# Expert inputs of a routed MoE: turned by VectorE after a round trip through HBM instead of by TensorE

## The chip, the cores and the metric

One NeuronCore of a Trainium2 chip runs the whole program. The metric is device time in microseconds (us). The kernel before took a median of 859.29 us over three runs (854.42 to 859.76).

The engines are named as the profile names them: PE is TensorE (matrix products; PEld its weight loads), DVE is VectorE, ACT is ScalarE, POOL is GpSimd, SP is SyncE. SP only issues DMAs here. A name with a q (SPq) is the instruction queue of that engine. Every engine works through its own instructions in the order in which the program wrote them; an instruction that waits holds up all that stand behind it on that engine.

## The reference

First an attention with a sigmoid in place of a softmax, then a mixture of eight experts to which the tokens are dealt out by a global sort.

```python
scores = scale * np.matmul(q, k.transpose(0, 1, 3, 2)) - np.log(S)     # batch 8, heads 12, S 448, head_dim 64
attn = 1.0 / (1.0 + np.exp(-scores)); x = attn @ v                      # as rows: 3584 tokens x 768
order = np.argsort(-(x @ w_gate).flatten())                             # E = 8 experts, cap = 3584 // 8 = 448
for idx in order:                                                       # best pair of token and expert first
    tok, e = idx // E, idx % E
    if assigned[tok] >= 0 or counts[e] >= cap: continue
    assigned[tok] = e; counts[e] += 1
for e in range(E):
    mask = assigned == e
    out[mask] = np.maximum(x[mask] @ w1[e], 0.0) @ w2[e]                # w1 768x1024, w2 1024x768
```

Each expert therefore gets exactly 448 tokens.

## The kernel before

**Stages.** The attention runs first and writes its result, one row of 768 numbers per token, to an HBM tensor `xs`. Within a row the columns stand in a permuted order (a, r, j): 4 quarters a, 6 blocks r, 32 columns j. Then come the eight experts in the order in which they fill up. "Expert k" below is the k-th of that order, counted from 0.

**An expert** (`moe`, from L833) is 288 products on PE, and a few more for experts 0 and 7. All numbers are split into a high and a low part in fp32r, so that each product of a pair takes three matmuls: high by high, low by high, high by low. The first half (products 0 to 143, L853 to L857) has the x of the expert as the moving operand, `xh` and `xl`, 448 tokens wide, with the features on the partitions. The second half (products 144 to 287, L890 to L894) has the hidden layer as the moving operand. The very first product of an expert reads all 448 columns of `xh`, the second all of `xl`.

**The weights** come in units, 8 in the first half and 6 in the second. SP loads a unit three units ahead (`load_w`), ACT rounds it to its high part (L709), POOL subtracts to get the low part (L711; VectorE does every second one from unit 84 on, which is in expert 6). POOL also makes the low part of the hidden layer (L865).

**x of the next expert.** Once the list of its 448 tokens is known, `prepare` puts these steps on the list of chores: four gathers of up to 128 rows of `xs` on POOL (`gather`, L731); a copy on ACT that puts a row's columns in order (`order`, L740); and eight `xturn`s. Each `xturn` is three 128x128 transposes on PE into PSUM (L757), a rounding copy to `xh` on ACT (L760), and a subtraction on VectorE to `xl` (L761). The fourth block of tokens has 64 rows.

**y of an expert** leaves PSUM by a VectorE transpose (`turn_y`, L787), is stored to an HBM tensor by SP (L793), read back in rows by SP (L797) and scattered to the output by POOL (`scatter`, L809), all in the course of the next expert.

**The router** finds the next expert and its tokens while an expert runs. `phase` is a generator: keys, a transpose on PE (`ends`, L178), nine steps of a search on VectorE (`grid_search`: each counts the keys over three thresholds, L185 to L240), then `prove` (PE transposes and counts, L289 and L290; VectorE reads a value into its sequencer and branches on it, L302, to an exact search of 16 passes if the count isn't 448), `choose`, `place` (L333 to L344) and `lists` (L356 to L374, with 32 small matmuls at L365). For expert 0 the search has four steps with a matmul in each (L230), and nothing else runs beside it.

**The order of the work** is written out by the program itself. A clock counts 189 ns for each product that is issued (L764). Each `yield` of the router names the time after which its next part is issued; SLACK, 150 ns, is added. Each chore has a due time; one chore is issued at a time, at least 1000 ns apart, the first of the list that is due. A due time of t is therefore a place in the stream of products: product t/189 of the expert. When an instruction really runs is decided by its engine's queue and by what it waits for.

The buffers that matter: `xr` has 12 (rows gathered and rows of y in turn), `xq` 2, `xh` and `xl` 2 each, the raw and split weights 4 each, the product's PSUM tile 2.

Of the kernel before, what the change touches and what calls it, by code (L numbers as in the profile page):

```python
# [7 lines left out]
F32 = mybir.dt.float32  # L8
# [23 lines left out]
T_GRID, T_PROVE, T_FOUND = (0, 2290, 3600, 3600, 3600, 3600, 3600), 3000, 9000  # L32
# [6 lines left out]
Y_WAIT, Y_LATE = 5000, 26000  # L39
N_FIRST, N_FAST = 4, 9  # L40
PAD = 176
NONE = 1.0e30
FOUND = 0x43E00000
ORDER = 2500

# [83 lines left out]
class Router:  # L129
# [217 lines left out]
    def lists(self):  # L347
# [13 lines left out]
        yield T_OH  # L361
# [38 lines left out]
    def phase(self, k):  # L400
        if k:
            self.remove()
        if k < 7:
            self.keys()
            yield T_KEYS
            self.ends()
            yield from self.grid_search(k)
            yield T_PROVE
            self.prove(k)
            yield T_FOUND  # L410
        else:
            self.left()
            yield T_PICK
        yield from self.place()
        yield from self.lists()


def moe_attention(tc, q, k, v, w_gate, w1, w2, out):
# [7 lines left out]
    with contextlib.ExitStack() as ctx:  # L426
# [14 lines left out]
        ys = [dr.tile([S, DM], F32, name=f"ys{i}") for i in range(2)]  # L441
        K = Consts()
# [118 lines left out]
        def scale():  # L561

            a = rw.tile([128, CP], F32, name="s_a", bufs=1)
            nc.vector.tensor_scalar(a.bitcast(I32), LE[:, 0].bitcast(I32), 0x7FFFFFFF, None, OP.bitwise_and)
            m = rw.tile([128, 2], F32, name="s_m", bufs=1)
            nc.vector.tensor_reduce(m[:, :1], a, AX.X, OP.max)
            p = ps_t.tile([128, 512], F32, name="tp")
# [9 lines left out]
            nc.vector.tensor_scalar(K.T0, K.kw[:, 0], K.base0, None, OP.add)  # L577

# [30 lines left out]
        for i in range(NPR + 1):  # L609
# [26 lines left out]
            if old and old[1] == NP - 1:  # L636
# [3 lines left out]
                if b == 3:  # L640
                    bg.append(scale)
# [81 lines left out]
        xg, xq, XH = {}, {}, {}  # L723
# [9 lines left out]

        def order(kx, j, n):

            xq[kx, j] = xp.tile([128, DM], F32, name="xq", bufs=2)
            to = xq[kx, j][:n].rearrange("p (r a j) -> p r a j", r=ND, j=32)
            of = xg[kx, j][:n].rearrange("p (a r j) -> p r a j", r=ND, j=32)
            if kx:
# [42 lines left out]
        def turn_y(kx, i, py, yr):  # L782
# [17 lines left out]
            if i == (2 if kx < E - 1 else 1):  # L800
                for j, n in blocks():
                    chores.append((clock[0] + 2 * wait, kx + 2, lambda j=j, n=n: rows_back(j, n)))
                for j, n in blocks() if kx < E - 1 else ():
                    chores.append((clock[0] + (Y_LATE if kx < E - 2 else 4 * wait) + 2000 * j, kx + 2,
# [133 lines left out]
        t_route, t_chore = FIRST, 1500.0  # L938
        for kx in range(E):
# [3 lines left out]
            def prepare():  # L943
                t0 = clock[0]
                lag = max(ORDER + 5000, min(14000, start + 40000 - t0))
                for j, n in blocks():
                    if kx:
                        chores.append((t0 + 1500 * j, kx + 1, lambda j=j, n=n: gather(kx + 1, j, n)))
                    else:
                        gather(1, j, n)  # L950
                bl = list(blocks())
                chores.append((t0 + lag - ORDER, kx + 1, lambda: order(kx + 1, *bl[0])))
                for i, (j, n) in enumerate(bl):
                    def first(i=i, j=j, n=n):
                        xturn(kx + 1, j, n, 0, False)
# [3 lines left out]
                    chores.append((t0 + lag + 1500 * j, kx + 1, lambda j=j, n=n: xturn(kx + 1, j, n, 1, False)))  # L959
# [6 lines left out]
            for step, cost in enumerate(moe(kx)):  # L966
# [4 lines left out]
                if t >= t_route:  # L971
# [43 lines left out]
```

## Time and profile before

| | |
|---|---|
| median of 3 runs | 859.29 us |
| the profiled execution: its time | 858.42 us |
| its span, first to last instruction | 856.6 us |
| mean granted TensorE clock | 0.978 of full speed |
| PE busy | 93% of the span |
| VectorE busy | 59% |
| POOL busy | 54% |
| ACT busy | 48% |

The profile is of one execution. "Busy" leaves out register, branch, semaphore and DMA-issuing instructions. Matmuls overlap: a product of 448 columns is shown with about 0.36 us, while the next one starts 0.20 us after it. So the distance from start to start is what counts on PE. The first product of expert 0 starts at 312.7 us, those of experts 1 to 7 at 388.3, 453.1, 521.6, 588.1, 655.3, 724.2 and 787.6 us, and the last product ends at 848.9 us.

### The profile page before, as it was taken

To read this page: it belongs to the slowest core of one execution; us is meant where nothing else is said; L and a number is where in the kernel's file an instruction comes from. 1 tells how busy PE (TensorE), PEld (TensorE's weight loads), DVE (VectorE), ACT (ScalarE), POOL (GpSimd) and SP (SyncE) were. 2 spreads that over 40 slices of the span, in tenths; PEclk is the share of its full clock that TensorE was granted. 3 is DMA by queue.
4 is the path that set the end of the run, shared out by engine and by line. 5 is a ranking of instruction groups with operands and counts; after the bars stand their busy time and mean duration, and the time that the engine had idled before them with its cause. 6 is when DMAs were issued, how large, how long until landed. Compare 5 with 4: busy or idle time off the path is not lost.

```text
span 856.6 us, 15002 instructions
## 1 busy us (share of the span) xinstructions
PE 800.2 (93%) x5151; PEld 614.3 (72%) x5151; DVE 504.3 (59%) x1439; ACT 408.4 (48%) x506; POOL 466.3 (54%) x446
## 2 busy tenths in 40 slices
PE   6999999999999259989999989999999999999996
PEld 3454554454544149879889879888888879889996
DVE  4676666666663779587487587387468433232150
ACT  6778777677775133433443332433433424551420
POOL 9744444344420035745865864874883795372561
PEclk9999999999999669999999999999999999999999
DMA  9787877778770261355576456555574565845743
GB/s 174 165 181 152 184 174 153 171 165 160 172 156 10 79 198 54 116 180 178 171 206 180 151 165 197 170 188 172 155 226 128 175 214 145 245 142 142 219 136 129
DMA packets 259705, 138.71 MB, mean 162 GB/s; under 512 B 187136, under 2 KB 248832, under 8 KB 259616
## 3 DMA queue, kind: packets, MB, share of 16 engines
q1 hardware_dynamic: 246880, 104.14, 47.6%
q0 software_dynamic: 10880, 33.28, 12.7%
q8 instruction: 41, 0.67, 0.3%
q10 hardware_dynamic: 1856, 0.23, 0.2%
q14 instruction: 48, 0.39, 0.2%
HBM read 105.02 MB, written 32.57 MB: 161 GB/s over the span
## 4 chain that ended last, share of the span: by engine, by line
PE 46%; DVE 9%; issue 3%; POOL 3%; DMA 2%; ACT 1%; SPq 0%; POOLq 0%; another core or an unknown queue 0%; DVEq 0%; ACTq 0%
PE sc L857 9%; PE sc L855 9%; PE sc L853 9%; PE sc L894 6%; PE sc L890 6%; PE sc L892 6%; PE tp L757 2%; POOL wl L711 2%; DMA xr<-xs,r_idx 1%; DVE r_oh L360 1%; PE rt L365 1%; POOL out_dram L809 1%; DVE r_junk L185 1%; DVE r_T L210 1%; DVE xl L761 1%
## 5 line engine op out<-in xcount | busy, mean ns | idle before, releaser
L711 POOL TENSOR_TENSOR wl<-wr,wh 128x768 fp32r<-128x768 f32 (+1 forms) x96 | 204.2, 2139 | 74.6 <-ACT wh L709 74.3
L502 ACT ACTIVATE at<-sc,bias 128x896 f32<-128x896 f32 x168 | 161.5, 1003 | 43.1 <-PE sc L512 25.6
L462 POOL DMA_DIRECT2D nkq<-in_q_dram x188 | 118.2, 643 | 115.2 <-DVE kqT L487 107.9
L894 PE MATMUL sc<-hh,wl 128*128 128x448 f32 (+2 forms) x400 | 147.6, 369 | 0.0
L890 PE MATMUL sc<-hh,wh 128*128 128x448 f32 (+2 forms) x400 | 145.3, 363 | 0.4 <-ACT yt L822 0.4
L857 PE MATMUL sc<-xh,wl 128*128 128x448 f32 (+2 forms) x396 | 145.6, 368 | 0.0
L855 PE MATMUL sc<-xl,wh 128*128 128x448 f32 (+2 forms) x396 | 144.9, 366 | 0.0
L853 PE MATMUL sc<-xh,wh 128*128 128x448 f32 (+2 forms) x396 | 144.8, 366 | 0.0
L892 PE MATMUL sc<-hl,wh 128*128 128x448 f32 (+2 forms) x400 | 144.4, 361 | 0.0
L709 ACT ACTIVATE wh<-wr 128x768 fp32r<-128x768 f32 (+1 forms) x112 | 101.5, 937 | 89.5 <-PE sc L892 56.1
L865 POOL TENSOR_TENSOR hl<-yt,hh 128x896 fp32r<-128x896 f32 x32 | 68.8, 2149 | 97.7 <-ACT yt L864 85.8
L536 PE MATMUL tp<-at,nv 128*64 128x448 f32 x576 | 118.8, 548 | 0.0
L861 ACT ACTIVATE hh<-sc 128x896 fp32r<-128x896 f32 x32 | 29.4, 919 | 146.8 <-PE sc L857 140.4
L496 DVE TENSOR_TENSOR kqL<-kqT,kqH 128x896 fp32r<-128x896 f32 (+1 forms) x49 | 52.5, 1073 | 57.1 <-ACT kqH L495 56.9
L892 PEld LDWEIGHTS sc<-hl,wh 128*128 128x128 f32 x400 | 77.6, 194 | 4.7 <-issue 1.1
L890 PEld LDWEIGHTS sc<-hh,wh 128*128 128x128 f32 x400 | 77.7, 194 | 3.8 <-ACT yt L822 0.6
L855 PEld LDWEIGHTS sc<-xl,wh 128*128 128x128 f32 x396 | 75.9, 192 | 6.3 <-issue 0.2
L894 PEld LDWEIGHTS sc<-hh,wl 128*128 128x128 f32 x400 | 77.6, 194 | 3.7
L853 PEld LDWEIGHTS sc<-xh,wh 128*128 128x128 f32 x396 | 76.1, 192 | 5.7
L857 PEld LDWEIGHTS sc<-xh,wl 128*128 128x128 f32 x396 | 76.0, 192 | 5.8
L536 PEld LDWEIGHTS tp<-at,nv 128*64 128x64 f32 x576 | 37.0, 136 | 59.2 <-issue 57.6
L731 POOL DMA_INDIRECT xr<-xs,r_idx x32 | 30.9, 965 | 71.8 <-ACT wh L709 59.2
(187 smaller groups left out, 1117.2 us busy)
## 6 DMA issues: line engine op xcount, KB each, us to landing
wr<-in_moe_w_dram SPq DMA_DIRECT2D x64, 384.0 KB
wr<-in_moe_w_dram SPq DMA_DIRECT2D x48, 512.0 KB
nkq<-in_k_dram SPq DMA_DIRECT2D x192, 56.0 KB
nkq<-in_q_dram POOLq DMA_DIRECT2D x188, 56.0 KB, 2.9
ys<-yt SPq DMA_DIRECT2D x92, 112.0 KB
xs<-xz SPq DMA_DIRECT2D x28, 336.0 KB
nv<-in_v_dram SPq DMA_DIRECT2D x92, 96.0 KB
xr<-ys SPq DMA_DIRECT2D x21, 384.0 KB
```

Source lines behind the costliest of these rows:

```text
L462: qn.dma_start(t[o:o + 32, n], rws[x])
L502: nc.scalar.activation(a, p[:, :, :S], AF.Sigmoid, bias=bias, scale=1 / math.sqrt(D))
L536: nc.tensor.matmul(p[j * 64:j * 64 + 64, :S], nat["v", b, g][:, h0 + j, c, :], AT[b, pr, c][:, j, :], start=(c == 0), stop=(c == 2 and pr ...
L709: nc.scalar.activation(hi, raw[u], AF.Copy)
L711: eng.tensor_tensor(lo, raw[u], hi.bitcast(F32), OP.subtract)
L853: nc.tensor.matmul(ph[:, f, lo:hi], wh[:, a, fs], xh[:, dd, lo:hi], start=st, stop=False)
L855: nc.tensor.matmul(ph[:, f, lo:hi], wh[:, a, fs], xl[:, dd, lo:hi], start=False, stop=False)
L857: nc.tensor.matmul(ph[:, f, lo:hi], wl[:, a, fs], xh[:, dd, lo:hi], start=False, stop=en)
L865: nc.gpsimd.tensor_tensor(h2, h0, h1.bitcast(F32), OP.subtract)
L890: nc.tensor.matmul(py[:, d2, :w], wh[:, a, dsl], h1, start=st, stop=False)
L892: nc.tensor.matmul(py[:, d2, :w], wh[:, a, dsl], h2, start=False, stop=False)
L894: nc.tensor.matmul(py[:, d2, :w], wl[:, a, dsl], h1, start=False, stop=(j == 1 and a == 3))
```

## The change

- For experts 2 to 7, `order` and `xturn` are gone. The gathered rows are written to a new HBM tensor `xd` by SP (`put_rows`), and read back by SP in another shape (`get_blocks`: four DMAs for each pair of blocks, one for each group of 32 partitions). VectorE then turns a block of 128 tokens in 32x32 blocks with one instruction (`xturn_dve`), ACT copies to `xh`, and VectorE subtracts to `xl`, now from two operands in SBUF. The turned block is written into the buffer of the gathered rows.
- These steps have due times from X_AT, 29500 ns into the expert before, or from the time at which the list is known if that is later: gathers at 0, 1500, 3000 and 4500 ns after it, writes from 5000, reads at 9500 and 12500, turns from 12500 on. They are sorted by due time; of two with the same time the one named first stays first.
- Search steps have a pitch of 16 products for lists 3 to 6 (20 before) and of 12 for list 2 (20 before); for lists 3 and later 1000 ns are added to the times after the keys and before the small matmuls of `lists`.
- Scatters are due from 23000 ns at 1500 ns (before: from 26000 at 2000), which is in the first half of the next expert.
- The search for expert 0 has three steps (before: four).
- Expert 1 is still turned by PE. While that goes on the router is held.
- The scale of the keys is worked out in two parts instead of one, and its scratch tile is one of the router's. `xq` holds two blocks in each buffer, and the pad shrinks.

```diff
-T_GRID, T_PROVE, T_FOUND = (0, 2290, 3600, 3600, 3600, 3600, 3600), 3000, 9000
+T_GRID, T_PROVE, T_FOUND = (0, 2290, 2100, 2850, 2850, 2850, 2850), 3000, 9000
+T_LATER = 1000
-Y_WAIT, Y_LATE = 5000, 26000
-N_FIRST, N_FAST = 4, 9
-PAD = 176
+Y_WAIT, Y_LATE = 5000, 23000
+N_FIRST, N_FAST = 3, 9
+PAD = 32
+HOLD_NS = 1000
+X_AT, X_PUT, X_GET, X_TURN = 29500, 5000, 9500, 12500
...
-        yield T_OH
+        yield T_OH + (T_LATER if k > 2 else 0)
...
-            yield T_KEYS
+            yield T_KEYS + (T_LATER if k > 2 else 0)
...
+        xd = [dr.tile([S, DM], F32, name=f"xd{i}") for i in range(2)]
...
+        def put_rows(kx, j, n):
+            nc.sync.dma_start(xd[kx % 2][128 * j:128 * j + n], xg[kx, j][:n])
+
+        def get_blocks(kx, g):
+
+            z = xz[kx, g] = xp.tile([128, 2, DM], F32, name="xq", bufs=2).rearrange("p h (b c) -> p (h b) c", c=192)
+            nb = min(8, S // 32 - 8 * g)
+            v = xd[kx % 2][256 * g:256 * g + 32 * nb].rearrange("(b t) (a c) -> a t b c", t=32, a=4)
+            for a in range(4):
+                nc.sync.dma_start(z[32 * a:32 * a + 32, :nb], v[a])
+
+        def xturn_dve(kx, j, n):
+
+            if j == 0:
+                XH[kx] = (xp.tile([128, ND, S], F32R, name="xh", bufs=2),
+                          xp.tile([128, ND, S], F32R, name="xl", bufs=2))
+            xh, xl = (x[:, :, j * 128:j * 128 + n] for x in XH[kx])
+            x = xg[kx, j][:, :ND * n].rearrange("p (r t) -> p r t", r=ND)
+            nc.vector.transpose(x.rearrange("p r (b t) -> p b r t", t=32),
+                                xz[kx, j // 2][:, j % 2 * 4:j % 2 * 4 + n // 32].rearrange("p b (r i) -> p b r i", i=32))
+            nc.scalar.activation(xh, x, AF.Copy)
+            nc.vector.tensor_tensor(xl, x, xh.bitcast(F32), OP.subtract)
...
-                    chores.append((clock[0] + (Y_LATE if kx < E - 2 else 4 * wait) + 2000 * j, kx + 2,
+                    chores.append((clock[0] + (Y_LATE if kx < E - 2 else 4 * wait) + 1500 * j, kx + 2,
...
             def prepare():
+                if kx:
+                    t0 = max(clock[0], start + X_AT)
+                    todo = [(1500 * j, lambda j=j, n=n: gather(kx + 1, j, n)) for j, n in blocks()]
+                    todo += [(X_PUT + 1500 * j, lambda j=j, n=n: put_rows(kx + 1, j, n)) for j, n in blocks()]
+                    todo += [(X_GET + 3000 * g, lambda g=g: get_blocks(kx + 1, g)) for g in range(2)]
+                    todo += [(X_TURN + 1500 * j, lambda j=j, n=n: xturn_dve(kx + 1, j, n)) for j, n in blocks()]
+                    chores.extend((t0 + t, kx + 1, f) for t, f in sorted(todo, key=lambda x: x[0]))
+                    return
...
-                if t >= t_route:
+                if t >= t_route and (not hold["left"] or t < hold["from"]):
                     t_route = t + next(route, 0) + SLACK
```

More of the change, by code (lines that the diff above doesn't have):

```diff
@@ L345, in place, with lists @@
         self.sl = sl
-    def lists(self):
+    def lists(self, k):
         nc, K, wk, sl = self.nc, self.K, self.wk, self.sl
@@ L414, in phase @@
         yield from self.place()
-        yield from self.lists()
+        yield from self.lists(k)
 def moe_attention(tc, q, k, v, w_gate, w1, w2, out):
@@ L561, in scale @@
         def scale():
-            a = rw.tile([128, CP], F32, name="s_a", bufs=1)
+            a = rw.tile([128, 224], F32, name="r_KE")[:, :CP]
             nc.vector.tensor_scalar(a.bitcast(I32), LE[:, 0].bitcast(I32), 0x7FFFFFFF, None, OP.bitwise_and)
@@ L566, in scale @@
             nc.vector.tensor_reduce(m[:, :1], a, AX.X, OP.max)
+            yield
             p = ps_t.tile([128, 512], F32, name="tp")
@@ L577, in scale @@
             nc.vector.tensor_scalar(K.T0, K.kw[:, 0], K.base0, None, OP.add)
+            yield
         XR = {}
@@ L639, in moe_attention @@
                     bg.append(lambda b=b: logits(b, range(NP)))
-                if b == 3:
-                    bg.append(scale)
+                if b in (3, 4):
+                    scaled = scale() if b == 3 else scaled
+                    bg.append(lambda: next(scaled))
                 for c in range(NCH if b >= B - LATE else 0):
@@ L721, in stream @@
                 state["split"] += 1
-        xg, xq, XH = {}, {}, {}
+        xg, xq, xz, XH = {}, {}, {}, {}
         def blocks():
@@ L732, in gather @@
                                          in_offset=bass.IndirectOffsetOnAxis(ap=listed[kx][:n, j:j + 1], axis=0))
+        def put_rows(kx, j, n):
[16 more added lines that the diff above has]
+            nc.vector.tensor_tensor(xl, x, xh.bitcast(F32), OP.subtract)
         def order(kx, j, n):
-            xq[kx, j] = xp.tile([128, DM], F32, name="xq", bufs=2)
+            if j % 2 == 0:
+                xq[kx] = xp.tile([128, 2, DM], F32, name="xq", bufs=2)
+            xq[kx, j] = xq[kx][:, j % 2]
             to = xq[kx, j][:n].rearrange("p (r a j) -> p r a j", r=ND, j=32)
             of = xg[kx, j][:n].rearrange("p (a r j) -> p r a j", r=ND, j=32)
-            if kx:
+            if kx or j > 1:
                 nc.scalar.copy(to, of)
@@ L938, in moe_attention @@
         t_route, t_chore = FIRST, 1500.0
+        hold = {"from": 0.0, "left": 0}
         for kx in range(E):
@@ L946, in prepare, with turn_x @@
                 for j, n in blocks():
[L947 to L950, printed above, removed]
+                    gather(1, j, n)
                 bl = list(blocks())
+                hold.update({"from": t0 + lag - HOLD_NS, "left": 2 * len(bl)})
+                def turn_x(j, n, hf):
+                    xturn(kx + 1, j, n, hf, False)
+                    hold["left"] -= 1
                 chores.append((t0 + lag - ORDER, kx + 1, lambda: order(kx + 1, *bl[0])))
@@ L954, in first @@
                     def first(i=i, j=j, n=n):
-                        xturn(kx + 1, j, n, 0, False)
+                        turn_x(j, n, 0)
                         if i + 1 < len(bl):
@@ L958, in prepare @@
                     chores.append((t0 + lag + 1500 * j, kx + 1, first))
-                    chores.append((t0 + lag + 1500 * j, kx + 1, lambda j=j, n=n: xturn(kx + 1, j, n, 1, False)))
+                    chores.append((t0 + lag + 1500 * j, kx + 1, lambda j=j, n=n: turn_x(j, n, 1)))
             def flush(kx):
```

## The prediction

> **What bounds the kernel now.** I read the page's busy shares first (table above), then the busy time of each expert's stretch, then PE, POOL and VectorE in order of time within a stretch.
>
> ```profile
> 388.30:453.10 64.80, 64.51 (x354) 58.26 (x353) 43.27 (x182) 25.84 (x35) 46.68 (x31) 1.00 0.61 183
> 453.10:521.60 68.50, 64.93 (x355) 58.22 (x354) 48.17 (x190) 25.08 (x34) 46.35 (x31) 1.00 0.59 174
> 521.60:588.10 66.50, 65.22 (x354) 58.00 (x354) 44.42 (x190) 25.20 (x34) 45.88 (x30) 1.00 0.60 179
> 588.10:655.30 67.20, 65.19 (x354) 58.23 (x354) 43.02 (x176) 25.24 (x34) 45.92 (x30) 1.00 0.60 177
> 655.30:724.20 68.90, 66.93 (x390) 59.27 (x390) 31.54 (x99) 25.08 (x34) 46.80 (x31) 1.00 0.58 174
> 724.20:787.60 63.40, 62.11 (x313) 56.95 (x312) 18.20 (x18) 25.27 (x34) 31.70 (x22) 1.00 0.61 186
> ```
>
> These are experts 1 to 6, in which x of experts 2 to 7 is made; the columns are length, then busy PE, PEld, DVE, ACT, POOL (with counts), clock, DMA share, GB/s. PE sets the pace at full clock. Its idle time, length less busy, is 0.3, 3.6, 1.3, 2.0, 2.0 and 1.3 us: 10.5 us. The whole gain must come out of that and out of PE's transposes. So the question is whether x is still ready when its first product is due.
>
> **What is removed.** PE's order of time in expert 0:
>
> ```profile
> 372.69 0.36 PE L892 MATMUL sc<-hl,wh 128*128 128x448 f32 x1
> 372.89 0.37 PE L894 MATMUL sc<-hh,wl 128*128 128x448 f32 x1
> 373.10 0.49 PE L757 MATMUL tp<-ident,xq 128*128 128x128 f32 x3
> 373.34 0.46 PE L890 MATMUL sc<-hh,wh 128*128 128x448 f32 x1
> ```
>
> From start to start a product takes 0.20 us, with three transposes behind it 0.45: a group costs 0.25. Six experts with 8 groups make 48 x 0.25 = 12.0 us. If all idle time of the six stretches went too, that is 22.5 us, an upper bound for this part with the 1000 ns more before the small matmuls. The step of expert 0's search stands alone on the path:
>
> ```profile
> 286.02 0.19 PE L230 MATMUL rt<-r_cnt,c_G 128*128 128x3 bf16 x1 [1.80 <-DVE r_junk L185]
> 288.01 0.17 PE L230 MATMUL rt<-r_cnt,c_G 128*128 128x3 bf16 x1 [1.80 <-DVE r_junk L185]
> ```
>
> One step less saves 2.0 us. Sum of gains: 24.5.
>
> **Where the gathers really run.** POOL in expert 3 (starts at 521.6):
>
> ```profile
> 547.82 4.74 POOL L711 TENSOR_TENSOR wl<-wr,wh 128x1024 fp32r<-128x1024 f32 x2
> ...
> 553.81 2.80 POOL L865 TENSOR_TENSOR hl<-yt,hh 128x896 fp32r<-128x896 f32 x1
> 556.57 2.39 POOL L711 TENSOR_TENSOR wl<-wr,wh 128x1024 fp32r<-128x1024 f32 x1
> ...
> 569.07 0.90 POOL L731 DMA_INDIRECT xr<-xs,r_idx  x1 [0.30 <-issue]
> ```
> ```profile
> DMA to landing us min/median/max: 4.5/6.2/6.7
> ```
>
> From the weights at 547.82 to the last gather POOL has no pause: subtractions, four scatters and four gathers follow each other. The last gather goes out 47.5 us into the expert. After the change the same instructions stand before it, only in another order (scatters ahead of the hidden layer's last subtraction, all gathers behind the scatters), so I leave it at 47.5, although product 180, its due place, is at 180 x 0.203 = 36.5. In expert 6 VectorE takes two of the subtractions of 2.4 us, one of them on this path in full: about 44. In the kernel before, copy and transposes began as blocks landed and needed no further DMA. Now each block goes to HBM and back.
>
> **The new chain.** SP's times for DMAs of this size, from the chain at the end of the kernel (start, us, what):
>
> ```profile
> 838.08 0.48 SPq L793
> ...
> 839.19 2.13 DMA ys<-yt
> ...
> 841.83 2.86 DMA xr<-ys
> ```
>
> The last gather lands after 4.5 to 6.7; I take the middle, 5.6: 53.1 us. Its write and the first read are both due at 9500, and the write stands first, so on SP the first read waits behind the last write, and that for the last gather: 0.5 to issue, then four DMAs of 0.5: 55.6. The read lands in 2.1 to 2.9, taken as 2.5: 58.1. The second read follows with a wait for the last write, while VectorE has the first pair. The weight loads behind the waiting writes lose little, since they are early:
>
> ```profile
> SPq L702 <- POOL wl L711: 128.0, 34, 15.1
> ```
>
> Here SP waited 128 us at 34 loads for a free weight buffer. ACT loses copies and gains shorter ones; it is idle over half of each stretch.
>
> VectorE's part is the same triple as in the attention, there for 896 columns:
>
> ```profile
> 106.30 1.07 DVE L487 STREAM_TRANSPOSE kqT<-nkq 128x896 f32<-128x896 f32 x1
> 107.47 0.95 ACT L495 ACTIVATE kqH<-kqT 128x896 fp32r<-128x896 f32 x1 [0.92 <-DVE kqT L487]
> 108.45 1.09 DVE L496 TENSOR_TENSOR kqL<-kqT,kqH 128x896 fp32r<-128x896 f32 x1 [1.08 <-ACT kqH L495]
> ```
>
> VectorE waits for ACT in the middle, and whatever stands behind it waits too. 106.30 to 109.54 is 3.24 us; for 768 columns 3.24 x 768/896 = 2.8. Three blocks and a half-wide one (1.7) make 10.1, with one `turn_y` (1.0) between them 11.1. So x is complete at 58.1 + 11.1 = 69.2 us, in expert 6 at 65.7.
>
> **When x is needed.** The stretches without transposes (2.0 each) and without idle time end at 62.5, 62.9, 63.2, 63.2, 64.9 and 60.1 us. The waits of PE by this alone: 6.7, 6.3, 6.0, 6.0, 4.3, 5.6, together 34.9.
>
> **The search in between.** VectorE also has the router:
>
> ```profile
> 509.83 0.44 DVE L185 TENSOR_SCALAR_CACHE_REDUCE r_junk<-r_KE,r_T 128x224 bf16<-128x224 f32 x1
> ...
> 512.27 1.11 DVE L787 STREAM_TRANSPOSE yt<-sc 128x896 f32<-128x896 f32 x1
> ```
> ```profile
> 540.03 0.17 DVE L293 TENSOR_SCALAR r_few<-rt 128x8 f32<-128x8 f32 x1 [6.91 <-PE rt L290]
> ...
> 547.31 0.58 DVE L310 SCALAR_TENSOR_TENSOR r_w<-r_kr,r_km,c_rank 112x8 f32<-112x8 f32 x1 [4.94 <-DVEq L302]
> ...
> 549.87 0.19 DVE L326 TENSOR_SCALAR csum<-csum,r_c 1x1 f32<-1x1 f32 x1
> ```
>
> A step takes 512.27 - 509.83 = 2.4 us, `prove` with `choose` 550.1 - 540.0 = 10.0, half of it the branch. By the planner's clock a phase is now 256 products of an expert's 288, so each list's search moves 32 products (276 and 12 before) earlier per expert: list 3 starts its steps at product 192 of expert 1, list 4 at 160 of expert 2, list 5 at 128 of expert 3, list 6 at 96 of expert 4. The turns are at 240 to 258 in expert 1, at 231, 237, 243 and 249 after that. So between the blocks VectorE finds:
> - experts 1 and 2: one step, 2.4 more: waits 9.1 and 8.7.
> - expert 3: step 8 between the blocks, step 9 and the last count (0.5) behind them, and PE's part of `prove` at product 273, 3.0 us before the end, waits for these: 69.2 + 2.4 + 2.4 + 0.5 = 74.5 against 60.2: 14.3.
> - expert 4: `prove` at 241, between the second and third block: 79.2 against 63.2: 16.0.
> - experts 5 and 6: nothing: 4.3 and 5.6.
>
> Besides, expert 3 begins with steps 7 to 9 left over (3 x 2.4 + 0.5) while PE meets `prove` at product 17 (3.5 us): 4.2 more. Sum: 62.2 us.
>
> **The clock.** After its long idle time before the experts PE restarts slowly:
>
> ```profile
> 295.00:300.00 5.00, 0.74 (x3) 0.56 (x4) 4.20 (x15) 0.00 (x0) 0.00 (x0) 0.50 0.23 73
> 314.00:316.00 2.00, 2.00 (x12) 2.00 (x11) 1.93 (x4) 1.19 (x2) 1.97 (x2) 0.50 0.88 311
> ```
>
> The products started at 312.7 and still had 0.50 at 314 to 316: 3.3 us at half speed lose 1.7. After six waits that is 10 at most, 0 if the other engines' backlog hides it; I take 6. The Trainium skill ("TensorE: Matmul & The Clock Gate", Why this matters for your kernels) says that gaps of over about 3 us in the products bring the slow clock back; the row agrees for a gap of tens of us, and no run here yet shows a gap of 4 to 16. By it the full 10 would be paid.
>
> **The subtraction.** Its operands are now both in SBUF. The nearest rows are a weight subtraction on VectorE with POOL idle and the same form among the experts:
>
> ```profile
> 303.41 0.95 DVE wl L711
> ```
> ```profile
> L711 DVE TENSOR_TENSOR wl<-wr,wh 128x768 fp32r<-128x768 f32 x8 | 9.2, 1156 | 23.5 <-ACT wh L709 23.5
> ```
>
> Alone it takes 0.95, among the experts 1.16 on average. The 24 blocks would pay 24 x 0.2 = 5, at most a POOL subtraction of 2.4 each, 58. I put 0 in the sum and 5 in the range, as the mean is near the low end. The Trainium skill ("SBUF — State Buffer", Who interferes with whom) has the rule: a VectorE instruction with two SBUF inputs and a GpSimd one that reads SBUF exclude each other, the second stands until the first ends.
>
> At nothing: the scale in two parts (beside the attention), the hold (expert 1's turns need VectorE then; the search resumes behind them), the earlier scatters (POOL's sum is the same).
>
> **Sum**, against the profiled 858.4 (0.9 below the median of the runs): -24.5 + 62.2 + 6 = +43.7: **902 us**.
>
> **Rivals.**
> 1. The transfers hide. If the last gather went out by about 41 us, 6.5 earlier, x would be complete when needed in experts 1, 2, 5 and 6, and a looser search would do the rest: 858.4 - 24.5 = 834. For it: the due place is at 36.5. Against: POOL's unbroken row. 0.15.
> 2. Break-even: landings and reads at their low ends (1.1 + 0.4 less) and the search done before the blocks come: 34.9 - 6 x 1.5 = 25.9 against 24.5: 860. 0.08.
> 3. POOL as the new bound of VectorE, decided where a subtraction meets the weight's in most blocks: half of 58 on top: 931. 0.05.
> 4. The shorter first search doesn't end on 448 and falls into the exact one: 16 passes of 2.4 with nothing beside them, 902 + 39 = 941. By the reference's inputs the coarser threshold still holds exactly 448 keys of the first expert: 0.02.
>
> The forecast has 0.70. Its own range: landings, reads and writes at both ends, 6 x 1.5 each way, the clock's 0 to 10, idle time that stays (up to 8) and the 5: 887 to 928. To leave out no more than about 2 in 10, the range goes down past the break-even case and up to the third: **848 to 931**. Within 1% (8.6 us, about what a measurement tells from no change) is the second rival: 0.08; faster 0.15; slower 0.77.
>
> **What would show it.** PE idle before the first product of experts 2 to 7, ended by VectorE's subtraction to `xl`, 4 to 9 us, 14 to 16 around the end of experts 3 and 4; the last gather still 44 to 50 us into the expert; SP waiting at the writes; the granted clock below 1 after the waits. Gathers that go out near product 180 would make it wrong.

## The result and the profile after

| | before | after |
|---|---|---|
| median | 859.52 us (4 runs) | 937.11 us (4 runs, 933.95 to 938.38) |
| ratio | | 1.090, 95% interval 1.085 to 1.095 |
| the profiled execution: time, span | 858.42, 856.6 us | 938.28, 936.5 us |
| mean granted clock | 0.978 | 0.928 |

The change makes the kernel 9% slower. The forecast was 902 us with a range of 848 to 931, so the time lies outside it: the direction and the chain of waits came as forecast, the sizes did not. The span grew by 79.9 us, where the sum had 43.7. All medians are of fast runs, and of the four runs of "The three at once" below a slow one (905.1 us) is left out.

The busy time of each expert's stretch, in the kernel after (length, then busy PE, PEld, DVE, ACT, POOL with counts, granted clock, DMA share, GB/s):

```profile
388.70:464.80 76.10, 61.86 (x331) 56.03 (x329) 52.68 (x219) 21.02 (x26) 44.11 (x29) 0.93 0.67 193
464.80:545.80 81.00, 66.15 (x330) 59.41 (x330) 49.91 (x191) 21.83 (x27) 45.05 (x30) 0.90 0.60 171
545.80:635.50 89.70, 68.10 (x332) 59.71 (x333) 52.67 (x227) 23.45 (x28) 49.29 (x32) 0.87 0.59 172
635.50:715.50 80.00, 62.11 (x331) 55.98 (x329) 45.23 (x184) 20.46 (x25) 42.52 (x28) 0.92 0.63 183
715.50:794.10 78.60, 67.49 (x363) 59.26 (x363) 19.85 (x42) 21.74 (x27) 45.02 (x30) 0.91 0.61 176
794.10:864.00 69.90, 61.13 (x288) 56.36 (x288) 23.01 (x18) 21.81 (x27) 34.02 (x23) 0.94 0.69 209
```

Against the six rows of before, PE has 22 to 27 instructions fewer in each stretch; it did 24 transposes there (some records are missing on either side). Its busy time is 386.8 us in all, 2.0 less than before, at a clock that is below 1.00 in every row. Its idle time is 88.5 us, where it was 10.4. No other engine comes near the length of a stretch, so this is a chain of waits and not a new bound. PE's order of time shows it (start, us, instruction, and in brackets the idle time before it and what ended that):

```profile
464.76 0.74 PE L885 MATMUL sc<-xh,wh 128*128 128x448 f32 x1 [13.39 <-ACT xh L761]
545.77 0.74 PE L885 MATMUL sc<-xh,wh 128*128 128x448 f32 x1 [11.38 <-ACT xh L761]
629.89 0.47 PE L292 MATMUL rt<-ident,r_base 128*128 128x128 f32 x1 [16.50 <-DVE r_base L243]
715.46 0.74 PE L885 MATMUL sc<-xh,wh 128*128 128x448 f32 x1 [16.82 <-ACT xh L761]
794.09 0.74 PE L885 MATMUL sc<-xh,wh 128*128 128x448 f32 x1 [9.08 <-ACT xh L761]
864.03 0.74 PE L885 MATMUL sc<-xh,wh 128*128 128x448 f32 x1 [8.77 <-ACT xh L761]
```

Five times the first product of an expert waits for its x (line 885, ended by ACT's copy of the last block), and in expert 3 the small matmul of `prove`, at product 273, waits for the search behind the turns. The six waits are 75.9 us.

**One chain, link by link.** The chain of work that ended last, in order of time, for the x of expert 6 (start, us, what):

```profile
770.20 6.68 DMA xr<-xs,r_idx
776.90 0.47 SPq L742
...
777.48 0.52 SPq L750
...
779.09 0.45 SPq L750
```

The last gather goes out at 770.20, 54.7 us into expert 5, and lands after 6.68. Only then can SP issue its write (line 742), and the four DMAs of the first read (line 750) stand behind that until 779.54. VectorE's order of time goes on from there:

```profile
783.64 0.98 DVE L759 STREAM_TRANSPOSE xr<-xq 128x768 f32<-128x768 f32 x1 [17.89 <-DMA xq<-xd]
785.53 0.96 DVE L762 TENSOR_TENSOR xl<-xr,xh 128x768 fp32r<-128x768 f32 x1 [0.91 <-ACT xh L761]
786.40 0.97 DVE L759 STREAM_TRANSPOSE xr<-xq 128x768 f32<-128x768 f32 x1
788.28 0.96 DVE L762 TENSOR_TENSOR xl<-xr,xh 128x768 fp32r<-128x768 f32 x1 [0.91 <-ACT xh L761]
789.16 1.11 DVE L819 STREAM_TRANSPOSE yt<-sc 128x896 f32<-128x896 f32 x1
...
794.07 0.56 DVE L762 TENSOR_TENSOR xl<-xr,xh 128x384 fp32r<-128x384 f32 x1 [0.59 <-ACT xh L761]
```

VectorE stands 17.89 us for the read, which comes 4.1 us after its last DMA was issued. Four blocks then take from 783.64 to 794.63, 11.0 us, with ACT's copy in the middle of each.

**SP's queue and the loads behind it.** From the waits of SP in the kernel after (line, releaser: us in all, times, longest), and from the groups of instructions after and before the rows of ACT's copy of the weights (its idle time and what ended most of it come last):

```profile
SPq L742 <- DMA xr<-xs,r_idx: 109.7, 20, 15.4
```
```profile
L716 ACT ACTIVATE wh<-wr 128x768 fp32r<-128x768 f32 (+1 forms) x112 | 100.7, 935 | 144.5 <-DMA wr<-in_moe_w_dram 111.8
```
```profile
L709 ACT ACTIVATE wh<-wr 128x768 fp32r<-128x768 f32 (+1 forms) x112 | 101.5, 937 | 89.5 <-PE sc L892 56.1
```

SP stands 109.7 us at the writes for the gathers, and the weight loads behind them in its queue come late: ACT's copies of weights now wait 111.8 us for loads, where the most of their waits was for PE. It reaches PE at product 266 of experts 2, 3 and 5, by way of POOL's subtraction; one of the three:

```profile
780.26 0.48 PE L926 MATMUL sc<-hh,wl 128*128 128x448 f32 x1 [1.04 <-POOL wl L718]
```

**The clock.** The first microseconds of expert 2, from 464.8 us (columns as in the stretches):

```profile
464.80:468.00 3.20, 3.20 (x8) 2.64 (x9) 3.06 (x16) 2.11 (x3) 2.48 (x2) 0.50 0.00 0
468.00:470.00 2.00, 2.00 (x7) 1.74 (x6) 1.86 (x14) 0.00 (x0) 2.00 (x2) 0.50 0.00 0
470.00:472.00 2.00, 2.00 (x10) 1.82 (x9) 2.00 (x8) 0.00 (x0) 0.93 (x1) 0.80 0.00 0
```

PE is busy without a pause and still has half speed for about 6 us. Behind the six waits this takes 6.0, 3.5, 4.7, 7.9, 4.4 and 6.1 us; the shortest and the longest:

```profile
545.80:549.30 3.50, 3.50 (x9) 2.89 (x10) 3.36 (x18) 2.23 (x3) 2.77 (x2) 0.50 0.68 218
715.50:723.40 7.90, 7.90 (x21) 6.18 (x22) 5.17 (x11) 2.11 (x3) 5.38 (x3) 0.50 0.48 129
```

Two shorter pauses, of 2.56 and 1.75 us, bring 3.4 and 2.7 us more. So PE is busy at half speed for 32.6 us in experts 1 to 6 and for 6.1 in expert 7, and half of that is lost: 16.3 and 3.1 us.

### The profile page after: what moved, and what is told of

The parts are those of the page before. It is cut to its first block, busy times and chain, and to the rows that moved or that the text cites. A ratio compares the mean times of both kernels' runs of the same rounds, so it can differ in the third digit from the quotient of the medians.

```text
span 936.5 us, 14751 instructions
## 1 busy us (share of the span) xinstructions
PE 803.0 (86%) x5006; PEld 615.6 (66%) x5006; DVE 513.5 (55%) x1426; ACT 389.2 (42%) x458; POOL 464.9 (50%) x446
## 5 line engine op out<-in xcount | busy, mean ns | idle before, releaser
L885 PE MATMUL sc<-xh,wh 128*128 128x448 f32 (+2 forms) x396 | 151.9, 384 | 59.7 <-ACT xh L761 59.4
L716 ACT ACTIVATE wh<-wr 128x768 fp32r<-128x768 f32 (+1 forms) x112 | 100.7, 935 | 144.5 <-DMA wr<-in_moe_w_dram 111.8
L887 PE MATMUL sc<-xl,wh 128*128 128x448 f32 (+2 forms) x396 | 151.4, 382 | 0.0
L889 PE MATMUL sc<-xh,wl 128*128 128x448 f32 (+2 forms) x396 | 150.3, 379 | 0.0
L885 PEld LDWEIGHTS sc<-xh,wh 128*128 128x128 f32 x396 | 80.0, 202 | 68.6 <-ACT xh L761 61.3
L887 PEld LDWEIGHTS sc<-xl,wh 128*128 128x128 f32 x396 | 79.5, 201 | 8.4 <-DVE xl L762 1.5
L889 PEld LDWEIGHTS sc<-xh,wl 128*128 128x128 f32 x396 | 79.5, 201 | 6.4 <-issue 0.2
L718 DVE TENSOR_TENSOR wl<-wr,wh 128x768 fp32r<-128x768 f32 (+1 forms) x16 | 30.6, 1919 | 68.5 <-ACT wh L716 68.3
```

The costliest lines, as they stand in the source:

```text
L716: nc.scalar.activation(hi, raw[u], AF.Copy)
L718: eng.tensor_tensor(lo, raw[u], hi.bitcast(F32), OP.subtract)
L885: nc.tensor.matmul(ph[:, f, lo:hi], wh[:, a, fs], xh[:, dd, lo:hi], start=st, stop=False)
L887: nc.tensor.matmul(ph[:, f, lo:hi], wh[:, a, fs], xl[:, dd, lo:hi], start=False, stop=False)
L889: nc.tensor.matmul(ph[:, f, lo:hi], wl[:, a, fs], xh[:, dd, lo:hi], start=False, stop=en)
```

## The experiments

All ratios are to the kernel before on the same chip, with a 95% interval. They came in four groups, in which its median was 859.2 (turning kept, x path alone, first read ahead, no round trip), 857.6 (hold, halves, early gathers, extra products), 856.3 (the mixed kernels, three steps, scatters) and 856.9 us (three edits, last one, last two). The product numbers count an expert's products on PE, 288 in each. Gains in us are against the 937 us of the kernel after, which ran in none of these groups; since the kernel before differs by up to 3 us from group to group, so may they. Where that matters, the gain worked out from the ratios stands beside it.

### The parts of the change

**Turning kept.** All of the change but its main part: x of experts 2 to 7 is ordered by ACT and turned by PE as before.

```diff
-                if kx:
+                if False:
                     t0 = max(clock[0], start + X_AT)
...
```

> The whole change except its x path: experts 2 to 7 are turned by PE as before; closer search steps, earlier scatters and the shorter first search stay. Theory A (x comes too late over HBM and VectorE): the loss is gone, 2 us less for the shorter first search and a few us either way for the closer steps: 852 to 864 us. Rival B (the closer search steps overload VectorE, and the scatters hold up POOL): most of the loss stays, over 890.

Measured: 863.5 us, 1.0054 (1.0031 to 1.0076). So the way through HBM makes some 74 of the 78 us. The rest, meant to save time, costs 4. The largest wait is in expert 3 at product 175, the first one that reads the last hidden layer's low part:

```profile
567.06 0.48 PE L924 MATMUL sc<-hl,wh 128*128 128x448 f32 x1 [4.41 <-POOL hl L897]
```

POOL has the earlier scatters and gathers ahead of that subtraction.

**The x path alone.** The way through HBM with the planner's times of before: search pitch, four steps in the first search, scatters from 26000 ns, no hold.

```diff
-T_GRID, T_PROVE, T_FOUND = (0, 2290, 2100, 2850, 2850, 2850, 2850), 3000, 9000
+T_GRID, T_PROVE, T_FOUND = (0, 2290, 3600, 3600, 3600, 3600, 3600), 3000, 9000
...
-Y_WAIT, Y_LATE = 5000, 23000
-N_FIRST, N_FAST = 3, 9
+Y_WAIT, Y_LATE = 5000, 26000
+N_FIRST, N_FAST = 4, 9
...
```

> The x path over HBM alone, on the planner's times of the kernel before (steps every 20 products, scatters from 26000, four first steps, no hold). Theory A: POOL's gathers go out at the same places, so PE waits 9 to 14 us before six experts and runs at half clock for some us after each: 900 to 930. Rival B: at most 870.

Measured: 920.9 us, 1.0712 (1.0648 to 1.0776). The path alone costs 62 us. With the new planner's times the whole change costs 78. The steps every 16 products carry the search earlier from expert to expert, until `prove` meets the turns, which the forecast had for experts 3 and 4; with the pitch of 20 `prove` does not meet them in any expert. But by the two traces that meeting is the smaller part: the six waits are 72.6 us here and 75.9 in the kernel after, the other idle time of experts 1 to 6 is 4.8 and 12.5, and PE is busy at half speed for 31.2 and 38.7 us in experts 1 to 7.

**Three steps in the first search,** in the kernel before.

```diff
-N_FIRST, N_FAST = 4, 9
+N_FIRST, N_FAST = 3, 9
```

> The kernel before with three steps in the first search in place of four. By the prediction's term 2.0 us less, a ratio of 0.9977 (0.997 to 0.9985). Rival: what follows the search is not ready earlier, or the coarser threshold ends elsewhere: 0.999 to 1.001, or above 1.04 with the exact search.

Measured: 854.8 us, 0.9982 (0.9967 to 0.9997), 1.5 us less by the medians. The products start 2.2 us earlier, but in expert 0 PE now waits for `place`:

```profile
357.41 0.19 PE L333 MATMUL rt<-c_ones,r_mk 112*64 112x1 bf16 x1 [2.30 <-DVE r_ei L325]
```

The search is not what is late there. The first instruction of `choose`, with two operands in SBUF, takes 2.42 us, where it took 0.28 in the kernel before; the three rows are VectorE and POOL here, and VectorE in the kernel before:

```profile
352.94 2.42 DVE L310 SCALAR_TENSOR_TENSOR r_w<-r_kr,r_km,c_rank 112x8 f32<-112x8 f32 x1 [4.98 <-DVEq L302]
352.93 2.41 POOL L711 TENSOR_TENSOR wl<-wr,wh 128x1024 fp32r<-128x1024 f32 x1
```
```profile
353.53 0.28 DVE L310 SCALAR_TENSOR_TENSOR r_w<-r_kr,r_km,c_rank 112x8 f32<-112x8 f32 x1 [4.78 <-DVEq L302]
```

It ends 0.02 us after POOL's weight subtraction. In the kernel after the same instruction takes 2.19 us (351.38 to 353.57, POOL's subtraction ends at 353.54) and PE waits 2.27. The x path alone, with four steps, has this wait too, and the last expert only, with three, has not. So it hangs on whether the instruction falls behind a subtraction of POOL, and not on the number of steps.

**The scatters alone,** in the kernel before.

```diff
-Y_WAIT, Y_LATE = 5000, 26000
+Y_WAIT, Y_LATE = 5000, 23000
...
-                    chores.append((clock[0] + (Y_LATE if kx < E - 2 else 4 * wait) + 2000 * j, kx + 2,
+                    chores.append((clock[0] + (Y_LATE if kx < E - 2 else 4 * wait) + 1500 * j, kx + 2,
```

> The kernel before with the scatters due 3 us of the planner's clock earlier and 1.5 us apart (26 us and 2 us before). Theory A (the scatters pass the last hidden layer's subtraction on POOL, and PE waits for it at product 175): waits there of 1 to 5 us in experts 3 to 5, 3 to 8 us in all, 861 to 866 against 858. Rival B (the 4 us that the changed kernel with PE's turning lost come of the closer search steps): 857 to 860.

Measured: 862.7 us, 1.0077 (1.0047 to 1.0107). The size is A's, the place is not. No wait for the hidden layer's low part shows; PE waits in experts 2, 4 and 5 for VectorE's one-hot instruction of `lists`. That instruction and POOL's in the same time:

```profile
488.42 6.06 DVE L360 TENSOR_TENSOR r_oh<-c_io,r_rr 112x2048 f16<-112x2048 int16 x1
```
```profile
487.98 0.96 POOL L809 DMA_INDIRECT out_dram<-xr,r_idx  x1 [0.21 <-issue]
488.96 2.13 POOL L865 TENSOR_TENSOR hl<-yt,hh 128x896 fp32r<-128x896 f32 x1
491.05 2.33 POOL L711 TENSOR_TENSOR wl<-wr,wh 128x1024 fp32r<-128x1024 f32 x1
```

and in the kernel before the same instruction, once with POOL subtracting nothing and once at this place, and what POOL did at this place:

```profile
299.17 1.22 DVE L360 TENSOR_TENSOR r_oh<-c_io,r_rr 112x2048 f16<-112x2048 int16 x1
...
487.31 3.61 DVE L360 TENSOR_TENSOR r_oh<-c_io,r_rr 112x2048 f16<-112x2048 int16 x1
```
```profile
487.44 2.39 POOL L711 TENSOR_TENSOR wl<-wr,wh 128x1024 fp32r<-128x1024 f32 x1
```

In the kernel before it stood behind one subtraction of POOL, of 2.39 us: 1.22 and 2.39 are 3.61. With the earlier scatters it stands behind two: 1.22, 2.13 and 2.33 are 5.68 of the 6.06. It had begun 0.54 us before the first of the two, while POOL was still at a scatter, so that it is not enough to begin first.

### The pieces of the chain

**No round trip.** No writes to HBM, and the reads take fixed rows of the input. VectorE's turns then work on other rows than the expert's, so the output is not the reference's; every other instruction stays.

```diff
         def put_rows(kx, j, n):
-            nc.sync.dma_start(xd[kx % 2][128 * j:128 * j + n], xg[kx, j][:n])
+            pass
...
-            v = xd[kx % 2][256 * g:256 * g + 32 * nb].rearrange("(b t) (a c) -> a t b c", t=32, a=4)
+            v = xs[256 * g:256 * g + 32 * nb].rearrange("(b t) (a c) -> a t b c", t=32, a=4)
```

> Leaves out the writes to HBM and reads the blocks from fixed rows of xs instead (so x of experts 2 to 7 is not that of their tokens); VectorE's turns still wait for the gathers, as they write into the same buffers. Theory A: the round trip is 7 to 9 us of each wait; what is left is the search around experts 3 and 4, some 5 to 8 us each: 855 to 885. Rival B: the waits of experts 3 and 4 and of the search stay in full, over 900.

Measured: 876.1 us, 1.0190 (1.0102 to 1.0278). 61 of the 78 us go. PE's waits for ACT's x fall from 59.4 to 20.3 us (groups of instructions by form; the last figures are the idle time before the group):

```profile
L885 PE MATMUL sc<-xh,wh 128*128 128x448 f32 x372 | 140.8, 378 | 20.3 <-ACT xh L761 20.3
```

The waits at product 266 are gone as well, so these were loads behind the writes. What is left is 5.1 to 9.0 us in experts 1 to 4, where the search is on VectorE, and 0.6 and none in experts 5 and 6, where it is not.

**The first read ahead of the last write.**

```diff
-X_AT, X_PUT, X_GET, X_TURN = 29500, 5000, 9500, 12500
+X_AT, X_PUT, X_GET, X_TURN = 29500, 5000, 9400, 12500
```

> The first read is issued ahead of the last write (due at 9400 instead of 9500). Theory A: the first two blocks can be turned while the last block is still on its way, so x is complete about 5 us sooner before each of six experts: 937 less 25 to 35, 902 to 912. Rival C (the DMAs themselves are slowed by the traffic, or VectorE's own time is the bound): under 10 us are gained, 927 or more.

Measured: 926.0 us, 1.0771 (1.0699 to 1.0842), 11 less. Of the 25 to 35 expected a third came: the read still stands behind the third write, whose gather goes out 1.3 us ahead of the last, and it still has to land.

**The read in two halves.**

```diff
-            for a in range(4):
-                nc.sync.dma_start(z[32 * a:32 * a + 32, :nb], v[a])
+            for b in range(0, nb, 4):
+                for a in range(4):
+                    nc.sync.dma_start(z[32 * a:32 * a + 32, b:min(nb, b + 4)], v[a][:, b:min(nb, b + 4)])
```

> The changed kernel with each read of a pair of blocks issued in two halves, so that the first turn waits for 393 KB and not for 786 KB. Theory A (the read is late by the bytes that it moves, 786 KB in 4.5 us): the first turn starts about 2 us earlier, the six waits lose 1.5 to 2 us each; 922 to 930 us against 937. Rival B (a fixed time for each DMA and its issue): eight issues in place of four, no gain or up to 1 us more for each expert, 935 to 944.

Measured: 923.2 us, 1.0765 (1.0737 to 1.0792), 14 less (12 by the ratios): A. The six waits are 65.4 us where they were 75.9, 1.7 less each. A second set of four issues costs less than the half that the first turn no longer waits for.

**The search held during all turns.**

```diff
+                    hold.update({"from": t0 + X_TURN - HOLD_NS, "left": 4})
                     chores.extend((t0 + t, kx + 1, f) for t, f in sorted(todo, key=lambda x: x[0]))
...
```

(and the count goes down with each turn).

> The changed kernel with the search held while the four turns of VectorE are outstanding, in every expert and not in the first alone. Theory A (search steps between the turns push the last x back): the waits at the end of experts 3 and 4, 16.5 and 16.8 us, fall to 9 to 11, those of experts 1 and 2 by one step of 2.4 at most, the last two stay; 917 to 926 us against 937. Rival B (the turns are late by their data alone, the search only fills the time in which VectorE would stand): the waits stay within 2 us, 932 to 940.

Measured: 914.3 us, 1.0678 (1.0647 to 1.0709), 23 less by the medians and 19 by the ratios: A. The wait at the end of expert 3, 16.50 us at `prove`, has become

```profile
611.05 0.74 PE L885 MATMUL sc<-xh,wh 128*128 128x448 f32 x1 [7.34 <-ACT xh L761]
```

and the six waits are 50.8 us. So 25.1 us of them were the search's.

**The three at once.**

> The changed kernel with three of the edits at once: the search held during the turns, the reads in two halves, the first read ahead of the last write. If the three act on one chain, in which each takes its own piece, their gains add: 937 less 23, 14 and 11, that is 889, between 885 and 900. If something else ends the waits once one piece is shortened (the gathers on POOL), they overlap: 900 to 915.

Measured: 895.3 us, 1.0433 (1.0384 to 1.0482), 42 less, where the single gains add to 48; by the ratios 40 of 42. That is within the range for pieces of one chain: they add. The six waits are 37.0 us:

```profile
L886 PE MATMUL sc<-xh,wh 128*128 128x448 f32 x372 | 144.5, 389 | 37.0 <-ACT xh L762 37.0
```

### The clock

**Extra products in the waits.** 38 to 77 products that nobody reads, at the place of each long wait.

```diff
+            def warm(x, n):
+                p = ps_t.tile([128, 512], F32, name="tp")
+                for _ in range(n):
+                    nc.tensor.matmul(p[:, :S], x[:, 0, :128], x[:, 0, :], start=True, stop=True)
+
+            if kx in WARM:
+                warm(XH[kx - 1][0], WARM[kx])
...
```

> The changed kernel with extra products on PE whose result nobody reads, 38 to 77 of them at the place of each of the six long waits, so that PE works through all but about 1 us of the wait. Theory A (the low clock after a wait comes of PE standing still): no stretch at 0.5 after the six waits, 8 to 14 us less, 922 to 929 us against 937. Rival B (the low clock has another cause, as the transfers at the expert's change): it stays, 935 to 945.

Measured: 929.5 us, 1.0823 (1.0792 to 1.0854), 7.6 less: A, just below its lower end. The stretch behind the wait, which had 0.50, has

```profile
463.20:465.00 1.80, 1.68 (x7) 1.31 (x8) 1.76 (x9) 1.80 (x3) 1.07 (x1) 1.00 0.00 0
465.00:467.00 2.00, 2.00 (x12) 1.81 (x11) 1.89 (x13) 0.32 (x1) 2.00 (x2) 1.00 0.03 8
```

full speed at once, and so have three more. At the two ends of expert 3, pauses of 1.60 and 2.04 us are left, and the low clock is still there behind them:

```profile
543.80:547.20 3.40, 3.40 (x10) 3.02 (x11) 3.23 (x21) 1.49 (x2) 3.40 (x2) 0.50 0.46 155
```

It is PE's standing still that brings the low clock, and not the transfers at that time. PE's busy time at half speed falls from 38.7 to 13.4 us in experts 1 to 7, which is worth 12.7; why only 7.6 came is open.

### Where the chain has room

**Early gathers.** As soon as the list is there and 15 us have gone, ahead of the scatters.

```diff
-X_AT, X_PUT, X_GET, X_TURN = 29500, 5000, 9500, 12500
+X_AT, X_PUT, X_GET, X_TURN = 15000, 9000, 13400, 20000
```

> The changed kernel with x of the next expert gathered as soon as its list is there and 15 us of the planner's clock have gone (29.5 before), ahead of the scatters on POOL, the writes 9.0, the first read 13.4 and the first turn 20 us behind it. Theory A (the waits are those of a chain that starts too late): the last gather goes out by 30 to 38 us into the expert and not at 46 to 55, the waits of experts 2 to 7 fall to 0 to 3 us each, and the slow clock behind them goes; 850 to 875 us. Rival B (POOL has no room earlier: its subtractions come late and PE waits for them): PE stands at wl and hl for 3 us or more in each expert, 885 to 915.

Measured: 893.9 us, 1.0422 (1.0384 to 1.0461). The time is B's, the reason for the most part neither's. Where a list is early it goes as A says: experts 5 and 6 end without a wait. But list 2 comes at product 165 of expert 1 and list 3 at 133 of expert 2, so there the gathers can't go out sooner, and the waits of 15.1 and 10.2 us stay. B's wait is there, but over 3 us in expert 3 alone, where PE waits 4.46 us for the hidden layer's subtraction (0.5 to 2.0 in the others). The search at the ends of experts 3 and 4 keeps 6.2 and 5.4 us.

**Mixed, with and without the hold.** Expert 2's x by PE, the others' early, scatters from 28500 ns.

```diff
-                if kx:
+                if kx > 1:
                     t0 = max(clock[0], start + X_AT)
...
-Y_WAIT, Y_LATE = 5000, 23000
+Y_WAIT, Y_LATE = 5000, 28500
...
-X_AT, X_PUT, X_GET, X_TURN = 29500, 5000, 9500, 12500
+X_AT, X_PUT, X_GET, X_TURN = 15000, 8000, 12400, 17000
...
```

> The changed kernel with x of expert 2 turned by PE as before (its list is there at product 165 of expert 1 at the earliest), and x of experts 3 to 7 through HBM with gathers from 15 us of the planner's clock on, writes 8.0, first read 12.4 and first turn 17 us behind them, the search held during the turns, and the scatters from 28.5 us on (23 before), behind the last hidden layer's subtraction. Theory A (the change as such pays where the chain starts early enough): no wait over 2 us before experts 4 to 7, stretches of 61 to 64 us; with 78.5 and 69 for experts 0 and 1 a sum of 838 to 852 us against 858 before. Rival B (a wait for data, the search or POOL's results remains in most experts): 858 to 880.

> The same without the hold in the later experts. If the search between the turns costs what the traces show (6.2 and 5.4 us at the search's last step in experts 3 and 4 with early gathers), 8 to 12 us more than with the hold; if the hold costs more by later lists than it saves, less than with it.

Measured: 872.7 us, 1.0169 (1.0125 to 1.0214) with the hold, 874.8 us, 1.0211 (1.0180 to 1.0241) without; the intervals overlap. Theory A's 838 to 852 is out. Experts 6 and 7 run at 60 and 61 us, but with the hold expert 3 takes 79.1, 4 and 5 72.1 and 71.4. The waits are small and many, for instance

```profile
537.85 0.32 PE L292 MATMUL rt<-ident,r_base 128*128 128x128 f32 x1 [2.23 <-DVE r_base L243]
594.49 0.48 PE L926 MATMUL sc<-hh,wl 128*128 128x448 f32 x1 [1.75 <-POOL wl L718]
675.32 0.71 PE L885 MATMUL sc<-xh,wh 128*128 128x448 f32 x1 [4.02 <-DVE yt L819]
```

for the search, for a weight and for `turn_y`, which frees the PSUM bank behind VectorE's turns. Without the hold, the turns push `prove` back by 9.0 and 8.3 us in experts 3 and 4, while expert 5 takes 64.0. What the hold saves early it loses by later lists. Expert 3 with the hold:

```profile
524.10:603.30 79.20, 70.11 (x330) 61.69 (x330) 47.85 (x192) 23.37 (x28) 46.70 (x31) 0.90 0.62 185
```

PE is idle for 9 us, in four pauses of 1.75 to 2.46 us for the most part. Behind them, and behind the 2.75 us ahead of the expert, it is busy at half speed for 16.1 us, which costs another 8, almost as much again. How these waits hang together is not settled.

**The last two experts only.** Experts 2 to 5 by PE, 6 and 7 early through HBM, scatters from 28500 ns, the planner's times of after.

```diff
-                if kx:
+                if kx > 4:
                     t0 = max(clock[0], start + X_AT)
...
```

> The changed kernel with PE's turning for experts 2 to 5 and the early way through HBM for experts 6 and 7 alone, scatters at 28.5 us behind the last hidden layer's subtraction. Against the 863.5 of PE's turning throughout: 5 less by expert 3's wait at product 175, 2.3 and 2.9 less by experts 5 and 6; 851 to 856. Rival (the later scatters push expert 5's gathers or the hidden layer): 856 to 864.

Measured: 853.2 us, 0.9955 (0.9932 to 0.9978), in the expected range. The wait at product 175 of expert 3 is 0.71 us, where it was 4.41 with PE's turning throughout. Experts 5 and 6 take 64.5 and 61.3 us for 66.3 and 62.8, so 1.8 and 1.5 less, where 2.3 and 2.9 were expected.

**The last expert only,** with the planner's times of before and three steps in the first search.

```diff
-                if kx:
+                if kx > 5:
                     t0 = max(clock[0], start + X_AT)
...
```

> The kernel before with three steps in the first search, and only the last expert's x through HBM, from 15 us of the planner's clock of expert 6 on, where its list has long been there. Expert 6 takes about 60.0 us as in the two mixed kernels and not 63.4; with the 1.5 us of the shorter search 849 to 853 us against 858, a ratio of 0.994. Rival (the early transfers take from the rest of expert 6 or 7 what they save): 854 to 858.

Measured: 849.3 us, 0.9919 (0.9896 to 0.9942): as expected, and the fastest of all. Its stretch of expert 6, where x of expert 7 is made:

```profile
716.60:776.20 59.60, 58.75 (x290) 55.01 (x289) 23.33 (x18) 22.10 (x26) 33.45 (x23) 1.00 0.77 234
```

59.6 us, where it was 63.4; busy 58.75 for 62.11, and 0.85 idle for 1.3. Its list is there before the expert begins and no search is on VectorE. Of the 7.6 us by the medians these are 3.8, and the shorter first search alone gave 1.5; where the other 2.3 come from has no run of its own.

## Why the prediction was right and wrong

The sum was 36.2 us short of the growth of the span. Three steps failed: the data's share of the six waits, above all the landing of the read; the clock, which came out at twice the bound set for it; and the idle time that was to go. By its terms, from the two profiled executions:

| term | forecast | measured | short by |
|---|---|---|---|
| first search, up to the end of expert 0 | -2.0 | +0.4 | 2.4 |
| PE's transposes, experts 1 to 6 | -12.0 | -18.3 | -6.3 |
| the clock, experts 1 to 6 and expert 7 | +6 | +16.3 + 3.5 | 13.8 |
| six waits before the products and at `prove` | +58.0 | +75.9 | 17.9 |
| other idle time of experts 1 to 6 | -10.5 + 4.2 | +2.1 | 8.4 |

(Measured: products begin 2.9 us earlier and expert 0 is 3.3 longer; PE's busy time in the six stretches 386.8 for 388.9, with 16.3 lost by half speed, so that 18.3 are left for the transposes; expert 7 64.8 for 61.3, of which half speed explains 3.1; idle time beside the six waits 12.5 for 10.4.)

**Right.**
- The direction, and the mechanism: x comes late, in the order gathers, SP, read, VectorE. Without the round trip 61 of 78 us go.
- The place of the gathers, read from POOL's unbroken row: the last goes out 46 to 55 us into an expert, and where the end of the products moves back by slow products and other waits, so does it. In experts 1, 2, 4, 5 and 6 it is 14.2 to 15.4 us ahead of the last product's end; the forecast had 15.0 to 17.4.
- VectorE's triples: 11.1 us forecast with one `turn_y`, 11.0 measured.
- The search: 23.1 us of the forecast's waits, 25.1 by the run with the hold, with `prove` at products 273 and 241, and longest at the ends of experts 3 and 4.
- The subtraction at nothing, but for a reason that it didn't give. None of the 24 met one of POOL's that had begun before it, and the 18 of 768 columns took 958 ns on average. The price of the third rival is real, as the one-hot instruction shows: 6.06 us in place of 1.22. The Trainium skill ("SBUF — State Buffer", Who interferes with whom) has the rule, and these rows agree with it; the rival's condition, a meeting in most blocks, didn't come.

**Wrong.**
- *The read's landing*, 2.5 us from a transfer of one block at the kernel's end. Here four DMAs of 192 KB land together in 4.1 (after the last issue, 779.54 to 783.64), and in 3.9 to 5.7 in the six experts, 4.4 on average: 11.6 us more over six waits. So this step holds most of the 15.9 us by which the data's share (50.8 for 34.9) was too small, and half of the bytes ahead of the first turn took back 10.5 us. The landing of the gather was 6.68 in the chain shown, 1.1 above the middle that I took; and in expert 5 the gather itself came 2.6 later against the products.
- *"If all idle time of the six stretches went".* It went, and as much came back: products 98, 175 and 266 and `prove` at 17 wait for the search, for POOL and for a weight, 11.3 of the 12.5 us. Two of the costs that the prediction set at next to nothing are among them. The weight loads behind the waiting writes ("lose little") cost 3.7 us at product 266, and the earlier scatters, which stand ahead of the hidden layer's subtraction, 2.7 at product 175 (the x path alone, with the scatters at their old place, has no such wait). POOL's sum was the same, but not its order. With PE's turning kept this part is a loss of 4 us by itself.
- *The clock*, 6, and 10 at most, for 19.8 us. I took its length, 3.3 us, from the start of the experts; after the six waits it is 3.5 to 7.9 us, and the two shorter pauses bring it too. The extra products take back 7.6.
- *The first search step*: 1.5 us alone, and nothing here. Expert 0 is 3.3 us longer; 2.3 of it are the wait for `place`, with VectorE's instruction behind POOL's subtraction. The sum set such meetings at nothing, and looked for them at the blocks of x alone.
- *The transposes' worth*, 12.0 for 18.3 us, an error to the good that hides part of the others. I took the one interval in which the transposes stand, 372.89 to 373.34. The product behind it starts late as well:

```profile
373.64 0.37 PE L892 MATMUL sc<-hl,wh 128*128 128x448 f32 x1
```

It comes 0.30 us after the one before it, where 0.20 is usual, so this group costs 0.34. In experts 1 and 5 of the kernel before, where no transpose waits, the eight groups cost 3.1 us each time, and in expert 6 of the fastest kernel PE's busy time is 3.4 us less (58.75 for 62.11), where 2.0 was forecast.

The signs that the forecast named came: idle time before the first products (9 to 13 us where 4 to 9 was said), 16.5 and 16.8 around the ends of experts 3 and 4 (14 to 16), the last gathers 46 to 55 us into an expert (44 to 50), SP at the writes, and the low clock behind the waits.

## What to carry to other kernels

Before work is taken off the bound engine by a longer way through memory, count that way backwards from where its result is due: its start is set by the last thing that stands in the queue before it, here POOL's gathers, and not by its due time. A saving of 3 us per expert is worth it only for those experts whose list is known early; done for one expert of six, with the shorter first search, it gave 0.8%; for all six, with the new planner's times, it cost 9%. A transfer that waits on an in-order queue also delays what is behind it, so what "costs nothing" has to be looked up in the order of each queue that it joins. And a wait of PE is to be counted with the slow clock behind it: here 16.3 us beside 88.5 us of idle time in experts 1 to 6.

## What was unexpected of the hardware

A pause of 2.56 us was enough for the low clock. In expert 2 PE waits for `place`, and then has 0.52, 0.50 and 0.66 until 495 us, with PE busy throughout:

```profile
490.53 0.19 PE L336 MATMUL rt<-c_ones,r_mk 112*64 112x1 bf16 x1 [2.56 <-DVE r_ei L328]
```
```profile
491.20:492.60 1.40, 1.40 (x6) 0.95 (x5) 0.26 (x2) 0.00 (x0) 0.00 (x0) 0.52 0.79 195
492.60:494.00 1.40, 1.40 (x5) 1.23 (x5) 1.23 (x6) 0.00 (x0) 0.00 (x0) 0.50 0.90 296
494.00:495.00 1.00, 1.00 (x5) 0.90 (x4) 1.00 (x2) 0.16 (x1) 0.00 (x0) 0.66 0.10 34
```

The Trainium skill ("TensorE: Matmul & The Clock Gate", Why this matters for your kernels) speaks of gaps over about 3 us; here shorter ones did it. Not every time, though: 1.75 us ahead of product 266 of expert 3 was followed by 0.51 from 610.7 to 614.1, but 2.27 and 2.35 us ahead of 355.61 and 553.57 by full speed. So these traces show no single length from which on a pause brings the low clock.

And a long VectorE instruction with two operands in SBUF can stand behind several of POOL's subtractions, one after the other: beside the 6.06 us above, VectorE's own weight subtraction of 1024 columns took 5.66 us at 829.34, while POOL did two of 2.13 and 2.40. A short one can as well: 0.28 us became 2.42.
